# Seven block products for the upper halves too in slices 11 to 14, two more fast steps, and the FFN's input made in another way

## The chip, the cores and the metric

The kernel runs on one core of one Trainium2 chip. The metric is device time in microseconds (us), the median of several runs. TensorE (PE) multiplies matrices, VectorE (DVE), ScalarE (ACT) and GpSimd (POOL) work element by element, and SyncE (SP) issues the DMA transfers, among them transposing ones.

## The reference

Three layers follow each other on 2304 tokens of 512 features (4 batches x 576 positions). The first is linear attention with 8 heads: softmax of q over the head's features, softmax of k over the positions, then q (k^T v). The second is a mixture of 8 experts in which all experts work on all tokens:

```python
P = np.exp(logits)                      # (2304, 8), balanced in 8 rounds over rows and columns
for e in range(E):
    h = np.maximum(x @ w1[e], 0.0)      # 512 -> 1024
    out += P[:, e:e + 1] * (h @ w2[e])  # 1024 -> 512
```

The third is a feed-forward layer (FFN) with a gate:

```python
h = x @ w_in                            # 512 -> 2048
g = h * np.clip(h + 3.0, 0.0, 6.0) / 6.0
return g @ w_out                        # 2048 -> 512
```

All arrays are f32.

## The kernel before

**Numbers in two halves.** Each f32 value on TensorE's way is two f16 values, an upper half (its rounding to f16) and a lower half (the rest). Of a product's four cross terms three are computed: upper x upper, upper x lower, lower x upper.

**Tiles and steps.** The tokens are 18 tiles of 128 (index j), six groups of three tiles (384 tokens), and three pairs of groups, `PAIRS`. The hidden features are cut into 20 slices s of 512: 0 to 15 are the experts' (`NE` = 16, two a expert), 16 to 19 the FFN's. A step (s, p) is one slice for one pair, 60 steps in all; `turns[s]` says in which order a slice takes the pairs (0,1,2 for odd slices and 16, mostly 2,1,0 for the others).

**First layer of a step (`ups`).** The product of x and w1 goes by Strassen's and Winograd's seven block products: 84 matmuls of 384 columns. Their results (banks x, y, z) are read by ACT and DVE into f32 tiles t[1] to t[4] (`ring_r`), put through relu, and split into an upper half (ACT) and a lower half (GpSimd or DVE), both in `ring_h`.

**Second layer (`downs`).** While a step's first layer runs, TensorE also works off the second layer of the step before, in pieces between the products. A plain step does it by `down_tile`: per token tile 12 matmuls of 512 columns, 72 a step, and one DVE operation that adds bank x factor to `acc` (128x512, all tokens stay in SBUF). In slices `FAST` (2 to 14 and 17 to 19) `downs_fast` takes a tile of both groups of the pair together, three times a step: `cross` forms seven block products of 4 matmuls of 256 columns for the two mixed terms, and `main` adds the upper x upper term in full, 8 matmuls of 256 and 4 of 512. The seven products need sums of the hidden features, `s_sums` (S, eight a step, one DVE operation on 128x768 f16 each, upper and lower halves summed apart), and sums of w2, `t_sums` (T1 to T4, once a slice, DVE on f16). ACT copies parts of banks on ("seeds"), and `onto` adds to `acc` by three DVE operations per tile. In the rows S appears as `xbuf<-ring_h`, T1 as scr, T2 as kvs, T3 as xbuf, T4 as xbuf and lg.

**Weights.** A slice's w1 and w2 come by DMA into one shared f32 buffer, `raw`, are scaled by a power of two and split into w1buf and w2buf (two of each). `when` says in which step they are asked for: w1 of the next slice in the first step of a slice, w2 in the second.

**The FFN's input.** When the mixture is done for a pair, in the steps after slice 15's last pieces, `x2_steps(p)` finds the largest value (`across_max`, with a small product by an identity), scales two groups of `acc` in place on ACT (`scaled`, 128x1536), takes three differences, and makes seven forms, each: upper half on ACT, lower half on GpSimd (three of them) or DVE, into one of three staging tiles in scr, then a transposing DMA on SP's queue into x's slot. For pairs 0 and 2 a store of the whole slot to DRAM (`xkeep`, 128x5376) ends the steps; seven loads (`reload`) bring x back in later slices.

**Order.** All operations are first recorded by a planner, which gives each a latest time by what needs it, lays every engine's list out in order of those times (an operation may stand up to `LEAD` = 40 us ahead of where the program recorded it, and "fill" operations such as weight work go where an engine has room), and then issues them. All of it is issued by line 469, so that nearly all rows of the profile carry L469. Each engine then works its list strictly in order. DVE and GpSimd aren't laid at the same time where they would share a port.

The lines that the change touches: `s_sums` and `t_sums` (1430, 1445), `down_tile` (1582), `ups` with its u0 to u6, `downs_fast` (from 1795), `x2_steps` (1944), `when` (2102), `after` (2155).

Of the kernel before, what the change touches and what calls it, by code (L numbers as in the profile page):

```python
# [71 lines left out]
class Planner:  # L72
# [23 lines left out]
    def __init__(self, nc):  # L96
# [5 lines left out]
        self.filling = False  # L102
        self.loose = 0.0
# [102 lines left out]
    def add(self, eng, name, a, k):  # L206
# [85 lines left out]
    def order(self):  # L292
# [14 lines left out]
        for o in ops:  # L307
            o["late"] -= EARLIER.get(o["mark"], 0.0)
# [5 lines left out]
    def lay(self, ops, first):  # L314
# [158 lines left out]
def tile_attention_moe_ffn(  # L473
# [30 lines left out]
    FAST = [*range(2, 15), *range(17, 20)]  # L504
    PAIRS = [(0, 1), (3, 4), (2, 5)]
# [86 lines left out]
    xs = [xbuf[:, i * X_W : (i + 1) * X_W] for i in range(len(PAIRS))]  # L592
    U = [scr[:, i * GN : (i + 1) * GN] for i in range(8)]
# [204 lines left out]
    def w2_steps(s, flat=raw):  # L798
# [12 lines left out]
        return steps + [sp(c) for c in range(NFC)]  # L811
# [618 lines left out]
    def s_sums(hs, which, qf):  # L1430

        a11, a12, a21, a22 = hs[1].get(qf + 2), hs[1].get(qf), hs[0].get(qf + 2), hs[0].get(qf)
        for k in which:
# [4 lines left out]
            elif k == 2:  # L1438
                nc.vector.tensor_sub(o, hs[2][1, qf], a11)
            elif k == 3:  # L1440
                nc.vector.tensor_sub(o, a11, a21)
            else:
                nc.vector.tensor_sub(o, a12, hs[2][2, qf])

    def t_sums(s, which):
        w = w2op[s % 2]
# [3 lines left out]
        for k in which:  # L1450
# [13 lines left out]
    def up_burst(s, p, qf, hs, between):  # L1464
# [57 lines left out]
        if not ffn:  # L1522
# [21 lines left out]
            if s in FAST:  # L1544
# [26 lines left out]
        if s in FAST:  # L1571
# [10 lines left out]
    def down_tile(s, p, grp, t, hs):  # L1582
        w = w2op[s % 2]
        g = PAIRS[p][grp]
        j = g * GJ + t
        ps = bank_of("d", [P, DM])
        ts_ = slice(t * P, (t + 1) * P)
# [7 lines left out]
        cf = factor(s, p, j)  # L1595
# [55 lines left out]

    def ups(s, p, hs):
# [3 lines left out]
        fast = s in FAST and (s, p) != order[-1]  # L1656
# [59 lines left out]
        def burst(qf):  # L1716
# [44 lines left out]
            def u5():  # L1761
# [6 lines left out]
                if fast:  # L1768
                    after_units(5, lambda: s_sums(hs, (3, 1), qf))
                    after_units(6, lambda: s_sums(hs, (2,), qf))  # L1770

            def u6():
# [11 lines left out]
                if fast:  # L1784
                    after_units(6, lambda: s_sums(hs, (4,), qf))
# [475 lines left out]
```

## Time and profile before

| | us |
|---|---|
| median of three runs | 1796.35 |
| the three runs | 1795.88, 1796.35, 1800.01 |
| the profiled execution, its own time | 1798.6 |
| its span, first to last instruction | 1796.8 |
| TensorE busy | 1773.1 (99%) |
| DVE, ACT, GpSimd busy | 1281.7, 1156.4, 551.5 |

The profile is of one execution; times inside it count from the first instruction. A step's start is the first matmul of 384 columns of its first layer. Slice 11 starts at 1003.71, slice 15 at 1340.51, step (16,0) at 1428.44 and (16,1) at 1457.26. The shown length of a matmul includes its way through the array, so what one costs in a stream is the distance of two starts.

### The profile page before, as it was taken

How to read it: one execution, taken by the hardware profiler on the slowest of the kernel's cores; microseconds unless marked ns; L12 is line 12 of the kernel's file. 1: busy time of each engine (PE TensorE's matmuls, PEld its weight loads, DVE VectorE, ACT ScalarE, POOL GpSimd, SP SyncE). 2: the span in 40 equal slices, each digit the busy share in tenths (PEclk: the TensorE clock that was granted, in tenths of full speed). 3: DMA queues.
4: the chain of work that ended last, by engine and by line, in shares of the span. 5: the costliest groups of instructions: out<-in, count | busy, mean ns of one | idle time of the engine just before them, and what ended most of it. 6: DMA issues, size and time to landing. Idle time of an engine off the chain costs nothing.

```text
span 1796.8 us, 32664 instructions
## 1 busy us (share of the span) xinstructions
PE 1773.1 (99%) x12917; PEld 1192.9 (66%) x12917; DVE 1281.7 (71%) x2379; ACT 1156.4 (64%) x2546; POOL 551.5 (31%) x530
## 2 busy tenths in 40 slices
PE   7999999999999999999999999999999989999999
PEld 5555556777777777777777777777776545577775
DVE  6874776787787778786867666665756786778774
ACT  5856575666676667676766666666656676776553
POOL 3423244323333242323232222222222433232221
PEclk9999999999999999999999999999999999999999
DMA  8410231423142323232322212020202563202031
GB/s 271 136 68 1 86 103 42 124 74 127 59 139 77 115 82 116 83 106 89 108 82 72 71 39 85 25 85 25 85 25 85 139 128 112 85 24 86 1 97 71
DMA packets 101593, 154.16 MB, mean 86 GB/s; under 512 B 47552, under 2 KB 51648, under 8 KB 100928
## 3 DMA queue, kind: packets, MB, share of 16 engines
q1 hardware_dynamic: 101440, 152.08, 27.1%
q8 instruction: 101, 1.65, 0.4%
q14 instruction: 52, 0.43, 0.1%
HBM read 119.69 MB, written 24.12 MB: 80 GB/s over the span
## 4 chain that ended last, share of the span: by engine, by line
PE 96%; DMA 1%; DVE 1%; ACT 1%; issue 1%; SPq 0%; POOL 0%; DVEq 0%
PE b L469 95%; PE b L2227 0%; DMA raw<-in_moe_w_dram 0%; DMA acc<-in_v_dram 0%; DMA xbuf<-in_k_dram 0%; DMA acc<-in_q_dram 0%; DVE acc L469 0%; ACT acc L469 0%; DVE prob L469 0%; SPq L469 0%; DVE ring_x2m L469 0%; DVE ring_c L469 0%; ACT ring_r L469 0%; ACT scr L469 0%; DVE ring_r L469 0%
## 5 line engine op out<-in xcount | busy, mean ns | idle before, releaser
L469 PE MATMUL b<-xbuf,w1buf 128*128 128x384 f16 x5040 | 906.6, 326 | 5.8 <-ACT ring_r L469 3.7
L469 PEld LDWEIGHTS <-w1buf 128*128 128x128 f16 x5040 | 492.3, 98 | 289.1 <-issue 7.9
L469 PE MATMUL b<-w2buf,ring_h 128*128 128x256 f16 (+1 forms) x3756 | 683.7, 315 | 0.0
L469 POOL TENSOR_TENSOR ring_h<-ring_r,ring_h 128x384 f16<-128x384 f32 x360 | 342.1, 952 | 1020.9 <-ACT ring_h L469 829.1
L469 PEld LDWEIGHTS <-ring_h 128*128 128x128 f16 x4320 | 422.1, 98 | 194.8 <-issue 3.0
L469 ACT COPY b<-b 128x256 f32<-128x256 f32 (+1 forms) x658 | 240.7, 374 | 291.8 <-PE b L469 193.3
L469 DVE SCALAR_TENSOR_TENSOR acc<-b,ring_cf,acc 128x512 f32<-128x512 f32 x369 | 275.3, 749 | 210.0 <-PE b L469 194.8
L469 ACT ACTIVATE ring_r<-b 128x384 f32<-128x384 f32 x432 | 210.9, 489 | 177.5 <-PE b L469 170.7
L469 PEld LDWEIGHTS <-xbuf 128*128 128x128 f16 x2436 | 225.0, 98 | 76.7
L469 DVE SCALAR_TENSOR_TENSOR ring_r<-b,ring_r 128x384 f32<-128x384 f32 x282 | 155.9, 553 | 119.2 <-ACT ring_r L469 58.1
L469 ACT ACTIVATE ring_h<-ring_r 128x384 f16<-128x384 f32 x330 | 168.8, 521 | 13.6 <-DVE ring_r L469 8.6
L469 DVE TENSOR_TENSOR xbuf<-ring_h 128x768 f16<-128x768 f16 x188 | 115.9, 617 | 1.7 <-POOL ring_h L469 1.7
L469 PE MATMUL b<-xbuf 64*64 64x65 f32 (+1 forms) x1140 | 96.8, 253 | 1.9 <-issue 1.2
L469 PE MATMUL b<-scr,xbuf 128*128 128x256 f16 x564 | 84.6, 273 | 0.0
L469 PE MATMUL b<-w2buf,xbuf 128*128 128x256 f16 x564 | 84.6, 273 | 0.0
L469 PE MATMUL b<-kvs,xbuf 128*128 128x256 f16 x564 | 84.6, 273 | 0.0
L469 ACT CAST ring_h<-ring_r 128x384 f16<-128x384 f32 x150 | 75.0, 508 | 10.4 <-DVE ring_r L469 9.5
L469 DVE SCALAR_TENSOR_TENSOR acc<-b,ring_co,acc 128x512 f32<-128x512 f32 x78 | 58.0, 748 | 32.2 <-PE b L469 30.2
L469 DVE SCALAR_TENSOR_TENSOR w1buf<-raw,ring_ws,w1buf 128x512 f16<-128x512 f32 x100 | 73.6, 768 | 3.0 <-ACT w1buf L469 2.4
L469 ACT ACTIVATE ring_r<-ring_r 128x384 f32<-128x384 f32 x114 | 59.6, 523 | 19.9 <-DVE ring_r L469 19.5
L469 ACT ACTIVATE w1buf<-raw,ring_ws 128x512 f16<-128x512 f32 x100 | 67.6, 714 | 6.1 <-DVE ring_ws L469 4.8
L469 DVE SCALAR_TENSOR_TENSOR ring_h<-ring_r,ring_h 128x384 f16<-128x384 f32 x96 | 63.9, 666 | 10.0 <-ACT ring_h L469 8.9
(167 smaller groups left out, 1554.7 us busy)
## 6 DMA issues: line engine op xcount, KB each, us to landing
xbuf<-xkeep SPq DMA_DIRECT2D x119, 384.0 KB, 3.7
raw<-in_moe_w_dram SPq DMA_DIRECT2D x31, 1024.0 KB, 6.5
xkeep<-xbuf SPq DMA_DIRECT2D x4, 2688.0 KB, 8.6
scr<-in_moe_w_in_dram SPq DMA_DIRECT2D x16, 512.0 KB, 3.6
scr<-in_moe_w_out_dram SPq DMA_DIRECT2D x16, 512.0 KB, 3.4
out_dram<-acc SPq DMA_DIRECT2D x18, 256.0 KB, 2.0
win<-scr SPq DMA_DIRECT2D x16, 256.0 KB, 2.6
wout<-scr SPq DMA_DIRECT2D x16, 256.0 KB, 2.1
```

Source lines behind the costliest of these rows:

```text
L469: f(*a, **k)
```

## The change

1. In slices `FULL` (11 to 14) `cross` takes all three terms through the seven products (6 matmuls each), and `main` does nothing. The sums S are made in f32 from the hidden tiles themselves (`whole`), in place, and then split, upper half on ACT and lower on DVE; the tiles take turns in twelve rooms (six of `ring_r`, six in scr). The sums of w2 are made in f32 in `raw` by four GpSimd operations and then split. One lower half per quarter (in `u6`) goes from GpSimd to DVE, with relu folded into its ACT operation. `raw` is thus in use longer, and `when` asks for the weights one step later in slices next to `FULL` ones.
2. The steps (15,0) and (16,2) (`ALSO`) also go by `downs_fast`. `onto` copies with ACT where `acc` is touched first.
3. x2: the scaling in place is gone. Each form scales while it makes its upper half, and its lower half is two DVE operations on 128x384, all seven on DVE. The store into `xkeep` is seven pieces, asked for after slice 16's steps (`keep`), and isn't laid ahead of its place (`patient`).
4. The very last token tile is cut in 384 and 128 columns, with a bank each.

The core of the diff:

```diff
+    ALSO = ((15, 0), (16, 2))
+    FULL = range(11, 15)
...
+        if s in FULL:
+            b11, b12, b21, b22 = w2_parts
+            steps += [lambda a=a: nc.gpsimd.tensor_sub(*a) for a in ((b11, b12, b11), (b12, b22, b12), (b22, b11, b22))]
+            steps += [lambda: nc.gpsimd.tensor_add(b21, b21, b22)]
...
     def t_sums(s, which):
+        if s in FULL:
+            b11, b12, b21, b22 = w2_parts
+            for k in which:
+                o, part = {1: (T1, b11), 2: (T2, b22), 3: (T3, b12), 4: (T4, b21)}[k]
+                split(o[0], o[1], part, res[s]["s2"][:, 0:1])
+            return
...
+        if (s, p, grp, t) == (*order[-1], 1, GJ - 1):
+            for cols in (slice(0, 3 * DM // 4), slice(3 * DM // 4, DM)):
+                ps = bank_of("d", [P, DM])[:, cols]
...
             def tile_(n):
-                t[n] = rt(f"r{n}_{s}_{p}_{qf}")
+                if full and rooms[0] % 12 > 5:
+                    t[n] = scr[:, rooms[0] % 12 % 6 * GN : (rooms[0] % 12 % 6 + 1) * GN]
+                else:
+                    t[n] = rt(f"r{n}_{s}_{p}_{qf}")
+                rooms[0] += 1
                 return t[n]
+
+            def whole(which):
+
+                for k in which:
+                    o = hs[2][k, qf] = sview[sums[0] % SN]
+                    sums[0] += 1
+                    if k == 1:
+                        r = t[1]
+                        nc.vector.tensor_add(r, t[4], r)
...
+                    else:
+                        r, other = (t[3], t[1]) if k == 2 else (t[4], t[4])
...
+                            nc.vector.scalar_tensor_tensor(
+                                out=r, in0=t[3], scalar=0.0, in1=other, op0=ALU.max, op1=ALU.subtract
+                            )
+                    nc.scalar.copy(o[:, 0, :], r)
+                    nc.vector.tensor_sub(o[:, 1, :], r, o[:, 0, :])
...
+                    if full:
+                        lo(hi(t[2], 1, qf, True), t[2], True)
+                        return
                     nc.scalar.activation(t[2], t[2], AF.Relu)
                     lo(hi(t[2], 1, qf, False), t[2], False)
...
             def cross(o, a, b, first=False):
...
+                terms = [(qf, x, y) for qf in range(2) for x, y in ((0, 1), (1, 0), (0, 0))[: 3 if whole_sums(s, p) else 2]]
...
             def main(o, grp, cols):
+                if whole_sums(s, p):
+                    return
...
-                nc.scalar.copy(o[:, 0], src)
-                eng.tensor_sub(o[:, 1], src, o[:, 0])
+                nc.scalar.activation(o[:, 0], src, AF.Copy, scale=by)
+                for c in range(2):
+                    eng.scalar_tensor_tensor(
+                        out=o[:, 1, c], in0=src[:, c], scalar=by, in1=o[:, 0, c], op0=ALU.mult, op1=ALU.subtract
+                    )
...
-            scaled(gb), sub(xtmp, b22, b12), form(QB22, b22, G), scaled(ga), sub(b12, b12, b11), form(QB11, b11, V),
-            sub(b22, b22, b12), form(QT3, xtmp, V), form(QB21, b21, G), form(QT1, b12, V),
-            sub(b21, b21, b22), form(QT2, b22, G), form(QT4, b21, V),
+        steps = [sub(xtmp, b22, b12), sub(b12, b12, b11)] + steps + [
+            form(QB22, b22, V), form(QB11, b11, V),
+            sub(b22, b22, b12), form(QT3, xtmp, V), form(QB21, b21, V), form(QT1, b12, V),
+            sub(b21, b21, b22), form(QT2, b22, V), form(QT4, b21, V),
         ]
-        if p in xkeep:
-            steps.append(lambda: nc.sync.dma_start(out=xkeep[p], in_=xs[(2, 1, 0)[p]]))
...
+    def keep(p, room):
+        n = X_W // 7
+        for i in range(7):
+            c = slice(i * n, (i + 1) * n)
+            nc.patient = True
+            nc.sync.dma_start(out=xkeep[p][:, c], in_=room[:, c])
+            nc.patient = False
...
-    when = {(s, turns[s][n]): ["w1", "w2"][n : n + 1] for s in range(2, NS - 1) for n in range(2)}
+    when = {
+        (s, turns[s][n + (s in FULL or s + 1 in FULL)]): ["w1", "w2"][n : n + 1]
+        for s in range(2, NS - 1) for n in range(2)
+    }
```

What it does to the order of instructions: first VectorE where step (11,2) ends and (12,2) begins, before. b_67 and b_66 are the banks of `onto`, b_65 the bank n1 and b_62 the bank y; `xbuf<-ring_h` is a sum S.

```order
L469 SCALAR_TENSOR_TENSOR acc<-b_67,ring_cf,acc 128x512
L469 SCALAR_TENSOR_TENSOR acc<-b_66,ring_cf,acc 128x512
L469 TENSOR_TENSOR xbuf<-ring_h 128x768
L469 TENSOR_TENSOR xbuf<-xbuf,ring_h 128x768
L469 TENSOR_TENSOR xbuf<-ring_h 128x768
L469 TENSOR_TENSOR xbuf<-ring_h,xbuf 128x768
L469 SCALAR_TENSOR_TENSOR acc<-b_65,ring_cf,acc 128x512
L469 SCALAR_TENSOR_TENSOR ring_r<-b_62,ring_r 128x384
L469 TENSOR_TENSOR ring_wsc<-ring_ws 128x1
L469 TENSOR_SCALAR ring_cf<-prob,ring_wsc 128x18
L469 SCALAR_TENSOR_TENSOR acc<-b_65,ring_cf,acc 128x512
L469 SCALAR_TENSOR_TENSOR ring_h<-ring_r,ring_h 128x384
```

The same place after the change.

```order
L471 TENSOR_TENSOR ring_r<-ring_r 128x384
L471 TENSOR_SCALAR ring_c1i<-ring_c_109 128x1
L471 TENSOR_SCALAR ring_ws<-ring_c1i 128x1 x2
L471 SCALAR_TENSOR_TENSOR ring_r<-b_62,ring_r 128x384
L471 SCALAR_TENSOR_TENSOR ring_r<-ring_r 128x384 x2
L471 SCALAR_TENSOR_TENSOR acc<-b_67,ring_cf,acc 128x512
L471 SCALAR_TENSOR_TENSOR acc<-b_66,ring_cf,acc 128x512
L471 TENSOR_TENSOR xbuf<-ring_r,xbuf 128x384 x2
L471 SCALAR_TENSOR_TENSOR ring_h<-ring_r,ring_h 128x384
L471 TENSOR_TENSOR xbuf<-ring_r,xbuf 128x384
L471 SCALAR_TENSOR_TENSOR ring_r<-ring_r 128x384
L471 SCALAR_TENSOR_TENSOR w2buf_82<-raw,ring_ws,w2buf_82 128x512 x2
```

Four f16 sums stood behind the two evictions from b_67 and b_66; now f32 operations in place (ring_r<-ring_r) stand ahead of the evictions, and the subtractions that make lower halves of S (`xbuf<-ring_r,xbuf`) behind them, with a lower half of h and w2 splits between.

SP's queue around the FFN's input, before. xkeep_96 is the store of pair 0 and xkeep_97 that of pair 2, win and wout are the FFN's weights.

```order
L469 DMA_TRANSPOSE xbuf<-scr 128x12x128
L469 DMA raw<-win_98 128x4x512
L469 DMA_TRANSPOSE xbuf<-scr 128x12x128 x6
L469 DMA xkeep_96<-xbuf 128x5376
L469 DMA_TRANSPOSE xbuf<-scr 128x12x128 x7
L469 DMA raw<-wout_99 128x4x512
L469 DMA_TRANSPOSE xbuf<-scr 128x12x128 x7
L469 DMA xkeep_97<-xbuf 128x5376
L469 DMA raw<-win_98 128x4x512
L469 DMA xbuf<-xkeep_96 128x768 x7
```

The same place after the change.

```order
L471 DMA_TRANSPOSE xbuf<-scr 128x12x128 x7
L471 DMA raw<-win_98 128x4x512
L471 DMA_TRANSPOSE xbuf<-scr 128x12x128 x14
L471 DMA raw<-wout_99 128x4x512
L471 DMA xkeep_96<-xbuf 128x768 x7
L471 DMA raw<-win_98 128x4x512
L471 DMA raw<-wout_99 128x4x512
L471 DMA xkeep_97<-xbuf 128x768 x7
L471 DMA xbuf<-xkeep_96 128x768 x7
```

The store of pair 0 stood between the transposes of two pairs; now it stands behind all 21 transposes, in seven pieces.

## Rows read from the trace of the kernel before

**Rows 1.** The page, part 1: busy time, share and instructions of each engine.
```profile
PE 1773.1 (99%) x12917; PEld 1192.9 (66%) x12917; DVE 1281.7 (71%) x2379; ACT 1156.4 (64%) x2546; POOL 551.5 (31%) x530
```

**Rows 2.** Waits of TensorE, whole span: total us, times, longest us.
```profile
PE b L469 <- DVE scr L469: 6.5, 2, 6.4
...
PE b L469 <- ACT ring_r L469: 3.7, 2, 3.0
```

**Rows 3.** Timeline of TensorE in slice 11: start, us, operation, count.
```profile
1003.71 2.11 PE L469 MATMUL b<-xbuf,w1buf 128*128 128x384 f16 x12
1005.66 0.60 PE L469 MATMUL b<-w2buf,ring_h 128*128 128x256 f16 x4
1006.09 2.11 PE L469 MATMUL b<-xbuf,w1buf 128*128 128x384 f16 x12
...
1013.49 1.03 PE L469 MATMUL b<-w2buf,ring_h 128*128 128x512 f16 x4
1014.35 0.38 PE L469 MATMUL b<-w2buf,xbuf 128*128 128x256 f16 x2
```

**Rows 4.** Windows: length, busy PE, PEld, DVE, ACT, POOL (count), clock, DMA share, GB/s.
```profile
1003.71:1087.91 84.20, 84.20 (x617) 59.98 (x614) 54.25 (x100) 52.79 (x123) 21.44 (x23) 1.00 0.19 59
496.10:582.48 86.38, 86.38 (x633) 61.58 (x631) 68.81 (x122) 59.34 (x137) 31.92 (x30) 1.00 0.34 112
1428.44:1457.26 28.82, 28.12 (x154) 14.74 (x151) 24.39 (x42) 20.88 (x33) 11.42 (x8) 1.00 0.79 190
1457.26:1493.43 36.17, 31.32 (x158) 15.79 (x158) 27.95 (x59) 28.00 (x49) 11.99 (x10) 0.95 0.58 126
1493.43:1522.62 29.19, 29.19 (x157) 15.27 (x156) 19.16 (x34) 19.55 (x39) 13.48 (x12) 1.00 0.31 119
```

**Rows 5.** Groups by form, VectorE, slices 11 to 14: count, busy us, mean ns, idle before.
```profile
L469 DVE TENSOR_TENSOR xbuf<-ring_h 128x768 f16<-128x768 f16 x48 | 27.7, 577 | 0.0
...
L469 DVE SCALAR_TENSOR_TENSOR ring_h<-ring_r,ring_h 128x384 f16<-128x384 f32 x24 | 17.1, 714 | 4.2 <-ACT ring_h L469 3.7
...
L469 DVE SCALAR_TENSOR_TENSOR w2buf<-raw,ring_ws,w2buf 128x512 f16<-128x512 f32 x16 | 11.6, 747 | 2.0 <-ACT w2buf L469 2.0
```

**Rows 6.** The same for ACT.
```profile
L469 ACT ACTIVATE ring_h<-ring_r 128x384 f16<-128x384 f32 x96 | 49.0, 522 | 3.4 <-DVE ring_r L469 1.5
...
L469 ACT ACTIVATE w2buf<-raw,ring_ws 128x512 f16<-128x512 f32 x16 | 10.6, 713 | 0.4
```

**Rows 7.** Timeline of VectorE where step (12,2) begins.
```profile
1085.94 0.56 DVE L469 SCALAR_TENSOR_TENSOR ring_r<-b,ring_r 128x384 f32<-128x384 f32 x1 [0.56 <-PE b L469]
1087.24 1.62 DVE L469 SCALAR_TENSOR_TENSOR acc<-b,ring_cf,acc 128x512 f32<-128x512 f32 x2 [0.74 <-PE b L469]
1088.78 0.55 DVE L469 TENSOR_TENSOR xbuf<-ring_h 128x768 f16<-128x768 f16 x1
```

**Rows 8.** Timelines of TensorE and of GpSimd at the same place.
```profile
1092.24 0.60 PE L469 MATMUL b<-kvs,xbuf 128*128 128x256 f16 x4
...
1087.68 0.91 POOL L469 TENSOR_TENSOR ring_h<-ring_r,ring_h 128x384 f16<-128x384 f32 x1 [0.68 <-ACT ring_h L469]
```

**Rows 9.** Timeline of TensorE in step (16,1); in brackets idle before and its releaser.
```profile
1461.32 2.13 PE L469 MATMUL b<-xbuf,w1buf 128*128 128x384 f16 x12 [1.89 <-DMA xbuf<-scr]
1466.40 1.59 PE L469 MATMUL b<-xbuf,w1buf 128*128 128x384 f16 x6 [2.96 <-ACT ring_r L469]
```

**Rows 10.** Timelines of SP's queue and of ACT around the same step.
```profile
1430.86 0.32 SPq L469 DMA_DIRECT2D xkeep<-xbuf  x1
1432.80 26.24 SPq L469 DMA_TRANSPOSE xbuf<-scr  x7
...
1460.50 1.58 ACT L469 ACTIVATE acc<-acc,sx 128x1536 f32<-128x1536 f32 x1 [2.56 <-DVE sx L469]
```

**Rows 11.** Groups by form, VectorE, whole span: lower halves of the x2 forms.
```profile
L469 DVE TENSOR_TENSOR scr<-acc,scr 128x768 f16<-128x768 f32 x9 | 9.1, 1009 | 0.0
```

**Rows 12.** Timeline of VectorE at the end of the span.
```profile
1793.13 0.75 DVE L469 SCALAR_TENSOR_TENSOR acc<-b,ring_co,acc 128x512 f32<-128x512 f32 x1 [1.84 <-PE b L469]
```

More of the change, by code (lines that the diff above doesn't have):

```diff
@@ L1585, in down_tile @@
         j = g * GJ + t
+        ts_ = slice(t * P, (t + 1) * P)
+        cf = factor(s, p, j)
+        if (s, p, grp, t) == (*order[-1], 1, GJ - 1):
+            for cols in (slice(0, 3 * DM // 4), slice(3 * DM // 4, DM)):
+                ps = bank_of("d", [P, DM])[:, cols]
+                for n in range(12):
+                    fc, (hi, wi) = (0, 2, 1, 3)[n // 3], ((0, 0), (0, 1), (1, 0))[n % 3]
+                    nc.tensor.matmul(ps, hs[grp][fc][:, hi, ts_], w[:, wi, fc, cols], start=(n == 0), stop=(n == 11))
+                nc.vector.scalar_tensor_tensor(
+                    out=acc[:, j, cols], in0=ps, scalar=cf, in1=acc[:, j, cols], op0=ALU.mult, op1=ALU.add
+                )
+            leave(s, j)
+            return
         ps = bank_of("d", [P, DM])
-        ts_ = slice(t * P, (t + 1) * P)
         n = 0
@@ L1655, in ups @@
         x = slot(s, p)
-        fast = s in FAST and (s, p) != order[-1]
+        fast = quick(s, p) and (s, p) != order[-1]
+        full = fast and whole_sums(s, p)
         ffn = s >= NE
@@ L1838, in onto @@
                 a = acc[:, j, :].rearrange("p (i n) -> p i n", n=hw)
-                nc.vector.scalar_tensor_tensor(
-                    out=a, in0=ps, scalar=factor(s, p, j), in1=a, op0=ALU.mult, op1=ALU.add
-                )
+                key = (j, s >= NE)
+                if key not in started:
+                    started.add(key)
+                    nc.scalar.activation(a, ps, AF.Copy, scale=factor(s, p, j))
+                else:
+                    nc.vector.scalar_tensor_tensor(
+                        out=a, in0=ps, scalar=factor(s, p, j), in1=a, op0=ALU.mult, op1=ALU.add
+                    )
             def p1():
@@ L1904, in begin @@
             d0[5]()
-        new = s != prev[0] and s in FAST
+        new = s != prev[0] and quick(s, p)
         T = lambda k: (lambda: t_sums(s, k) if new else None)
@@ L1961, in x2_steps @@
         )
[L1963 to L1964 removed]
+        by = sx[:, p, 0:1]
         def sub(o, u, v):
@@ L2160, in after @@
             if ps_ == NE - 1:
-                run(loosely(x2_steps(pp), X2_LATE[pp]))
+                run(marked(f, f"x2{pp}") for f in loosely(x2_steps(pp), X2_LATE[pp]) if f is not None)
                 done.add(("x2", pp))
+            if ps_ == NE and pp in xkeep:
+                keep(pp, xs[(2, 1, 0)[pp]])
     put(ticks, w1_1[4:])
@@ L2206, in tile_attention_moe_ffn @@
             all_conv()
-        fast = prev is not None and prev[0] in FAST
+        fast = prev is not None and quick(*prev[:2])
         if laid and not fast:
```

92 lines of the change are left out of this document (61 added, 31 removed).

## The prediction

> **What bounds the kernel now.** I read the page's first part first, then TensorE's waits, then the timeline and the windows of the stages that the change touches. TensorE is busy 1773.1 us of the span [rows 1], so all its idle time together is 23.7 us, and most of the named waits are elsewhere: 6.5 us while the kernel starts, and 5.6 us (3.7 behind ACT and 1.9 behind a transfer) between slices 15 and 16 [rows 2, 9]. In slices 11 to 14 it has none: slice 11 is 84.20 us with 84.20 busy [rows 4]. There the time is the number of matmuls times their spacing, and a slice gets shorter only if matmuls go or get narrower, as long as VectorE (DVE), at 54.25 us, keeps up.
>
> The spacing comes from the starts. Twelve matmuls of 384 columns take 1005.66 - 1003.71 = 1.95 us, so 162.5 ns each; four of 512 take 1014.35 - 1013.49 = 0.86 us, so 215 ns [rows 3]. For 256 columns I take the slice as a whole: 84.20 less 252 x 0.1625 and less 36 x 0.215 leaves 35.5 us for 324 matmuls, 109.6 ns each; the four at 1005.66 agree (0.43 us) [rows 3, 4].
>
> **Seven products for upper halves (slices 11 to 14).** Per token tile and pair of groups TensorE now issues 7 x 4 matmuls of 256 and for the upper halves 8 of 256 and 4 of 512: 36 x 0.1096 + 0.86 = 4.81 us. After the change it is 7 x 6 = 42 of 256: 4.60 us. That is -0.203 us, times 3 tiles, 3 pairs and 4 slices (36): **-7.3 us**, all on the path, because TensorE has no idle time there.
>
> What this costs beside TensorE: each of the 24 sums of a slice was one f16 operation of 577 ns at most [rows 5], and is now one f32 operation of 384 columns on DVE, one ACT copy and one DVE subtraction to f16. Neighbouring DVE operations start some 0.5 us apart, though each shows 0.55 (1088.78, 0.55, in a row of four) [rows 7], so a 384-column operation counts about 0.51, and a sum gains 0.51 us: 24 x 0.51 = 12.2. Six lower halves move from ACT and GpSimd to ACT and DVE, some 0.6 each by the row at 714 with its contention [rows 5]: 3.6. The four sums of w2 become four splits of 747 ns in place of five f16 sums; I take that as even. So DVE has 54.25 + 15.8 = 70 us in a slice of 84.20 - 1.8 = 82.4 (85%); with 714 ns for every subtraction and 0.56 for every f32 operation it is 77 (93%). Slice 5 runs today at 68.81 of 86.38 (80%) with TensorE never idle [rows 4]. ACT: 24 - 6 operations of 522 ns and four of 713 [rows 5, 6] add 12.2 to 52.79, 79%. By the totals both engines have room; the order decides.
>
> The tight place is the start of a step. DVE finishes its last read of a product at 1085.94 + 0.56, evicts two banks from 1087.24, makes the four sums from 1088.78, and TensorE first uses one at 1092.24 [rows 7, 8]. The changed order puts the f32 parts ahead of the two evictions and the subtractions behind them. Three subtractions from 1088.78 at 0.51 to 0.71 are done by 1090.3 to 1090.9, 1.3 us or more before 1092.24. The in-place f32 operation must however wait for GpSimd to have read its tile (a lower half ends there at 1087.68 + 0.91 = 1088.6 [rows 8]); then the two evictions (1.62) and three subtractions (1.5 to 2.1) stand behind it on the same engine: with the f32 operation 1088.6 + 0.56 + 1.62 + 1.5 to 2.1 = 1092.3 to 1092.9, up to 0.7 us late. I take **+1.0 us** over the twelve steps (the subtractions mostly in time, as the order puts GpSimd's reads early), with 0 and 12 x 0.7 = +8.4 as ends; a gain below 0 is excluded, since TensorE has nothing idle there to give back.
>
> **Slices (15,0) and (16,2) fast.** A plain step has 72 matmuls of 512 in its second layer, 72 x 0.215 = 15.48; a fast one 3 x 4.81 = 14.42. Two of them: **-2.1 us**. It adds eight f16 sums (some 0.5 each) and three evictions to DVE in each of the two steps.
>
> **The boundary of 15 and 16: x2 redone.** Here TensorE is idle 28.82 - 28.12 = 0.70 and 36.17 - 31.32 = 4.85 us, and the second window has a granted clock of 0.95, 36.17 x 0.05 = 1.8 us at the 1.2 GHz level behind the idle time; together 7.35 us to be had [rows 4]. The wait at 1461.32 is for a transposing DMA, the one at 1466.40 for ACT, which has scalings of 1.58 us on 128x1536 in its order there [rows 9, 10]. The store of x stands on SP's queue at 1430.86, directly ahead of the seven transposes of the next pair, which then take from 1432.80 to 1459.04 to be issued [rows 10]. The change takes both causes away: the scalings are folded into the forms, and in the changed order the store comes behind all transposes of the next two pairs.
>
> What it adds there is DVE work: seven forms with two half-width operations each, 14 x 0.51 to 0.71 = 7.1 to 10 us, in place of four subtractions of 1.009 [rows 11], since three were on GpSimd: +3.1 to +6 per pair, I take +4.5. DVE has 24.39 + 27.95 + 19.16 = 71.5 us in the three windows from 1428.44 to 1522.62 [rows 4]; with two pairs (9), the sums and evictions of (16,2) (some 6) it has 86.5, and if the whole 7.35 us came back there would be 94.2 - 7.35 = 86.8 for it. DVE would have to be full for three steps, in an order that also waits. So I take half, **-3.7 us**, between 0 and -7.35.
>
> **Last tile.** The final tile's product is cut into 384 and 128 columns. TensorE's total stays (12 x 0.215 against 12 x (0.1625 + about 0.054)); after its last matmul only 128 columns are to be added instead of 512, which took 0.75 us [rows 12]. By 0.56 for 384 columns some 0.3 remain: **-0.4 us**.
>
> **Sum.** -7.3 - 2.1 - 3.7 - 0.4 + 1.0 = -12.5 us. The profiled execution took 1798.6 us (1796.8 of span), 2.25 above the median of the three runs, so 1798.6 - 12.5 = 1786.1 on its scale is **1783.9 us** on the median's. The small edits (when a weight is asked for, first touches of the output on ACT, sign of a sum) are counted at nothing: raw is held one step longer, and by the order the next weights are still asked for a step (28 us) ahead of their first use. If that cover is gone, the first step of a slice waits.
>
> **Rivals.** (a) Nothing comes back at the boundary: DVE, fuller by 4.5 us a pair, becomes what TensorE waits for. For: the account above is full to 0.3 us. Against: most of the work may slide into the lighter steps before and after. 1783.9 + 3.7 = 1787.6 us.
>
> (b) The sums are late at each step's start by the 0.7 us worked out above. For: DVE takes its work in order, and waits for GpSimd where it did not. Against: 1.3 us of slack if GpSimd is early. 1783.9 + 7.4 = 1791.3 us.
>
> (c) Slower: DVE bounds the twelve steps. If it waits for every ACT copy before its subtraction with nothing in between, a sum costs 0.56 + 0.52 + 0.57 = 1.65 us instead of 0.51: 9.1 us more per step, and 1.2 for the lower halves, on the 18.1 us (54.25 / 3) of now: 28.4; two waits of 0.91 for GpSimd make it 30.2 against TensorE's 27.5. 12 x 2.7 = 32 us, so 1815 us. It decides from about 29.0 us a step (1.5 us late), where the sum passes +0.3%. Against: the changed order puts evictions and other tiles' work between copy and subtraction.
>
> (d) The narrow matmuls cost more than their columns in the new, longer groups of six. A tile costs 4.81 us before, so seven products pay only while one of 42 takes less than 4.81 / 42 = 0.1145 us; the rows show 0.1096 in groups of four [rows 3, 4], and eight percent would have to come from the grouping alone. At 0.1145 the 7.3 us are gone: 1783.9 + 7.3 = 1791.2 us. Nothing in the rows speaks for it; 1 in 100.
>
> The Trainium skill, page "TensorE: Matmul & The Clock Gate", section "Back-to-back issue gap", speaks against the change here: in a stream of weight loads and matmuls the sustained spacing is about 81 ns for 128 columns and 131 ns for 512, and the isolated formula N / 2.4 + 2.5 overstates wide ones. An estimate from that page (98 ns for 256 columns, between its two) would make a tile 4.05 us before and 4.12 after, +2.3 us over the 36 instead of a gain. This case's rows disagree, with 215 ns for 512 columns in just such a stream.
>
> **Chances.** Forecast and its own spread (1779 to 1787): 0.60; (a) 0.18; (b) 0.15, about half of it within the bound; (c) 0.04; (d) 0.01; that the weights, taken later, hold up a step so that most of the gain goes: 0.02. A measurement of this kernel tells about 0.3% (5.4 us) from no change, so faster means under 1791.0 and slower over 1801.7: faster 0.85, same 0.11, slower 0.04. The range goes from everything recovered (1783.9 - 3.65 - 1.0 = 1779.2, less some scatter: 1778.5) up to (b) with a little: 1792.
>
> **What would show it.** In the changed trace slices 11 to 14 should be 82.4 us, with DVE at 68 to 77 and no wait of TensorE for DVE; a row of waits behind a sum (xbuf) in those slices is (b), DVE above 80 is (c). Between 15 and 16 the transposes should no longer be spread over 26 us, ACT shows no scaling of 1.58 us, and idle time plus half clock should be about half of 7.35 us; if idle time there is behind DVE, it is (a). The steps after (15,0) and (16,2) should be 28.1 where plain ones are 29.1. The prediction is wrong if slices 11 to 14 do not get shorter by 1.8 us each, or if another boundary grows.

## The result, and the profile after

The changed kernel takes 1780.49 us, the median of five runs (1779.69 to 1781.37); before it were 1796.35. The ratio is 0.9905, with a 95% interval of 0.9891 to 0.992: faster, by 15.9 us, 3.4 us more than forecast and inside the range. All medians below are of fast runs; of e1 one run in four, at 3782.23 us, counts as slow and is left out. The profiled execution took 1781.37 us, its span is 1779.6.

The page's first part (after), which answers to [rows 1]: TensorE has 20.3 us of idle time in the span, against 23.7, and 1759.3 us of busy time, against 1773.1. So most of the gain is busy time that went; the table below says how much of that is matmuls and how much the lower clock.

```profile
PE 1759.3 (99%) x13097; PEld 1208.3 (68%) x13097; DVE 1377.2 (77%) x2550; ACT 1193.9 (67%) x2654; POOL 543.4 (31%) x513
```

Windows of the kernel after, columns as in [rows 4]: slices 12 and 13, steps (15,0) and (15,2), then the steps (16,0), (16,1) and (16,2).

```profile
1084.00:1166.57 82.57, 82.49 (x635) 61.73 (x632) 69.92 (x127) 61.68 (x147) 22.83 (x20) 1.00 0.20 60
1166.57:1248.89 82.32, 82.32 (x633) 61.74 (x632) 69.66 (x128) 61.40 (x147) 23.14 (x20) 1.00 0.20 60
1331.22:1360.03 28.81, 27.62 (x214) 20.61 (x211) 25.92 (x47) 21.70 (x52) 10.80 (x9) 1.00 0.27 83
1389.42:1418.67 29.25, 29.25 (x159) 15.33 (x157) 25.87 (x46) 14.47 (x25) 4.76 (x5) 1.00 0.63 124
1418.67:1447.92 29.25, 29.25 (x160) 15.33 (x158) 27.62 (x50) 16.68 (x30) 9.27 (x8) 1.00 0.52 98
1447.92:1478.07 30.15, 29.46 (x160) 15.39 (x159) 29.05 (x64) 23.06 (x39) 7.63 (x7) 1.00 0.58 97
1478.07:1507.69 29.62, 29.62 (x160) 15.50 (x159) 25.09 (x49) 23.73 (x48) 9.99 (x9) 1.00 0.49 164
```

Slices 12 and 13 last 82.57 and 82.32 us, where they were 84.20; VectorE is busy 69.9 and 69.7 us of that, ACT 61.7. Step (16,1) lasts 30.15 us instead of 36.17, at a granted clock of 1.00 instead of 0.95. Step (15,0) has 1.19 us without TensorE that weren't there before. Where a step starts among the pieces of the second layer has moved too, so single steps don't compare well: (15,1) takes 29.39 us, not the 28.1 that the prediction expected behind (15,0), but (15,1) and (15,2) together take 58.64 where they took 59.84.

TensorE's waits (after) from slice 11 to the end of slice 16, in all:

```profile
PE b L471 <- ACT ring_r L471: 1.2, 1, 1.2
PE b L471 <- DVE ring_r L471: 0.7, 1, 0.7
```

The first is the new wait in (15,0); the second, in (16,1), is what is left of the 5.6 us that [rows 2, 9] show there. From the start of slice 11 to the end of the span the traces differ by 793.09 - 777.32 = 15.8 us (1796.8 - 1003.71 and 1779.6 - 1002.28; before slice 11 they differ by 1.4, of which 1.2 arose in the first 243 us, which the change leaves alone). The 15.8 us split like this; matmuls are counted with the distance of starts in the longest runs of one width, the same in both traces (20 of 256 columns in 2.18 us, 109.2 ns each, and 12 of 512 in 2.59 us, 215.8 ns each):

| part | forecast, us | measured, us | from |
|---|---|---|---|
| FULL, matmuls | -7.3 | -7.5 | 36 x (4.794 - 4.586) |
| FULL, waits | +1.0 | +1.3 | 1.19 in (15,0) and 0.08 in slice 12 (82.57 - 82.49) |
| fast steps (15,0) and (16,2) | -2.1 | -2.3 | 2 x (15.54 - 14.38), matmuls |
| boundary of 15 and 16 | -3.7 | -6.7 | idle 5.55 to 0.69, and the 1.8 that the 1.2 GHz level cost |
| last tile | -0.4 | -0.3 | start of (19,0) to the end: 47.44 to 47.19 |
| sum | -12.5 | -15.5 | of 15.8; 0.3 are not assigned |

The start of step (12,2), which answers to [rows 7, 8]. TensorE's first use of a sum, VectorE ahead of it, and GpSimd's lower half that the f32 operation in place has to wait for (all after):

```profile
1089.87 0.82 PE L471 MATMUL b<-kvs,xbuf 128*128 128x256 f16 x6
1090.52 0.82 PE L471 MATMUL b<-xbuf 128*128 128x256 f16 x6
```

```profile
1084.67 1.14 DVE L471 SCALAR_TENSOR_TENSOR ring_r<-ring_r 128x384 f32<-128x384 f32 x2
1085.91 1.41 DVE L471 SCALAR_TENSOR_TENSOR acc<-b,ring_cf,acc 128x512 f32<-128x512 f32 x2
1087.24 1.02 DVE L471 TENSOR_TENSOR xbuf<-ring_r,xbuf 128x384 f16<-128x384 f32 x2
1088.17 0.55 DVE L471 SCALAR_TENSOR_TENSOR ring_h<-ring_r,ring_h 128x384 f16<-128x384 f32 x1
1088.64 0.55 DVE L471 TENSOR_TENSOR xbuf<-ring_r,xbuf 128x384 f16<-128x384 f32 x1
```

```profile
1083.04 0.91 POOL L471 TENSOR_TENSOR ring_h<-ring_r,ring_h 128x384 f16<-128x384 f32 x1 [3.65 <-ACT ring_h L471]
```

GpSimd's lower half ends at 1083.95, ahead of the operations in place at 1084.67, so that wait costs nothing here. Two sums' subtractions end at 1088.26, and TensorE uses the first at 1089.87: 1.6 us of slack, where 1.3 or more was forecast for the case of an early GpSimd.

The wait in (15,0) is the one place in slices 11 to 15 where the new sums hold TensorE. Timelines of TensorE, ACT, VectorE and GpSimd there (after):

```profile
1342.69 1.14 PE L471 MATMUL b<-xbuf,w1buf 128*128 128x384 f16 x6 [1.19 <-ACT ring_r L471]
```

```profile
1342.14 0.49 ACT L471 ACTIVATE ring_r<-b 128x384 f32<-128x384 f32 x1 [1.38 <-DVE xbuf L471]
```

```profile
1340.38 1.73 DVE L471 TENSOR_TENSOR xbuf<-ring_r,xbuf 128x384 f16<-128x384 f32 x2
```

```profile
1340.44 1.25 POOL L471 TENSOR_TENSOR ring_h<-ring_r,ring_h 128x384 f16<-128x384 f32 x1 [1.34 <-ACT ring_h L471]
```

Read backwards: TensorE waits for a bank that ACT reads; ACT's read at 1342.14 waited 1.38 us for VectorE, since the f32 tile that it writes was still the source of a sum's subtraction; the two subtractions took 1.73 us instead of 1.02 (1087.24 above), beside a GpSimd operation that took 1.25. That 0.7 us more is over half of the 1.19. FULL steps have twelve rooms for these tiles; by the diff an ordinary step such as (15,0) takes only the six of `ring_r`, so it comes back to a room sooner.

SP's queue around x2 (after), which answers to [rows 10]: all 21 transposes stand ahead of the first piece of the store (xkeep). The 14 are two sevens of 21.7 and 20.5 us, where they took 26.2 and 25.0. With the store put back (e2) the first of these sevens takes 22.1, so the store made little of the spread that the prediction put beside it.

```profile
1396.97 17.17 SPq L471 DMA_TRANSPOSE xbuf<-scr  x7
1414.19 0.90 SPq L471 DMA_DIRECT2D raw<-win  x1
1425.25 49.74 SPq L471 DMA_TRANSPOSE xbuf<-scr  x14
1478.92 0.38 SPq L471 DMA_DIRECT2D raw<-wout  x1
1479.35 4.59 SPq L471 DMA_DIRECT2D xkeep<-xbuf  x7
```

The x2 groups on VectorE, steps (15,2) to (16,2), after and then before: the new lower halves (36 of 42 in one group), and the differences on 128x768.

```profile
L471 DVE SCALAR_TENSOR_TENSOR scr<-acc,sx,scr 128x384 f16<-128x384 f32 x36 | 23.3, 692 | 0.0
...
L471 DVE TENSOR_TENSOR acc<-acc 128x768 f32<-128x768 f32 x9 | 8.8, 980 | 0.1
```

```profile
L469 DVE TENSOR_TENSOR acc<-acc 128x768 f32<-128x768 f32 x9 | 10.9, 1213 | 1.8 <-ACT acc L469 1.8
```

VectorE's last operations in the span (after), which answer to [rows 12]: two operations, 384 and 128 columns, 1.02 us together in place of 0.75, but the span ends sooner, because the first runs beside the last matmuls.

```profile
1775.50 1.02 DVE L471 SCALAR_TENSOR_TENSOR acc<-b,ring_co,acc 128x384 f32<-128x384 f32 x2 [1.20 <-PE b L471]
```

### The profile page after: what moved, and what is told of

Same layout as the page of the kernel before. It is cut to its first block, busy times and chain, and to the rows that moved or that the text cites. A ratio compares the mean times of both kernels' runs of the same rounds, so it can differ in the third digit from the quotient of the medians.

```text
span 1779.6 us, 33317 instructions
## 1 busy us (share of the span) xinstructions
PE 1759.3 (99%) x13097; PEld 1208.3 (68%) x13097; DVE 1377.2 (77%) x2550; ACT 1193.9 (67%) x2654; POOL 543.4 (31%) x513
## 4 chain that ended last, share of the span: by engine, by line
PE 96%; DVE 2%; DMA 1%; ACT 0%; issue 0%; SPq 0%; POOL 0%; ACTq 0%; POOLq 0%
PE b L471 96%; DMA acc<-in_v_dram 0%; DMA raw<-in_moe_w_dram 0%; DVE xbuf L471 0%; DMA xbuf<-in_k_dram 0%; DMA acc<-in_q_dram 0%; DVE ring_r L471 0%; PE b L2331 0%; DVE prob L471 0%; DVE ring_c L471 0%; DVE ring_h L471 0%; DVE ring_qm L471 0%; DVE scr L471 0%; SPq L471 0%; DVE acc L471 0%
## 5 line engine op out<-in xcount | busy, mean ns | idle before, releaser
L471 PE MATMUL b<-w2buf,ring_h 128*128 128x256 f16 (+1 forms) x3456 | 608.5, 310 | 0.1
L471 POOL TENSOR_TENSOR ring_h<-ring_r,ring_h 128x384 f16<-128x384 f32 x312 | 299.5, 962 | 876.5 <-ACT ring_h L471 727.3
L471 PEld LDWEIGHTS <-ring_h 128*128 128x128 f16 x4116 | 401.2, 98 | 171.6 <-issue 2.1
L471 PEld LDWEIGHTS <-xbuf 128*128 128x128 f16 x2820 | 262.9, 98 | 77.3
L471 ACT ACTIVATE ring_r<-b 128x384 f32<-128x384 f32 x384 | 187.5, 489 | 141.7 <-PE b L471 135.4
L471 PE MATMUL b<-xbuf 128*128 128x256 f16 (+1 forms) x1236 | 107.3, 249 | 4.1 <-issue 1.7
L471 DVE TENSOR_TENSOR xbuf<-ring_h 128x768 f16<-128x768 f16 x148 | 91.4, 620 | 0.0
L471 DVE SCALAR_TENSOR_TENSOR acc<-b,ring_co,acc 128x512 f32<-128x512 f32 (+1 forms) x82 | 60.5, 742 | 30.7 <-PE b L471 27.6
L471 PE MATMUL b<-xbuf,ring_h 128*128 128x256 f16 x366 | 80.0, 273 | 0.0
L471 PE MATMUL b<-lg,ring_h 128*128 128x256 f16 x294 | 74.1, 273 | 0.0
```

What stands on the lines that cost most here:

```text
L471: f(*a, **k)
```

## The experiments

Each kernel was timed in three rounds or more beside the kernel before on the same chip; a ratio is to that kernel. The medians come from several chips, so differences of medians are rough. Traces are compared from the start of slice 11 to the end of the span, which leaves out the kernel's start (it differs by some us between executions of one program): 793.1 us before, 777.3 after. That column is from one execution of each kernel. The intervals of e2 and e3 reach into that of the changed kernel, so that they cost anything rests on their traces.

| kernel | median, us | ratio to before (95%) | slice 11 to end, against after |
|---|---|---|---|
| after | 1780.49 | 0.9905 (0.9891 to 0.992) | 0 |
| e1 FULL out | 1788.81 | 0.9953 (0.9936 to 0.997) | +8.0 |
| e2 store put back | 1784.16 | 0.9921 (0.9905 to 0.9938) | +4.4 |
| e3 forms put back | 1784.73 | 0.9927 (0.9911 to 0.9943) | +2.3 |
| e10 fast steps out | 1784.80 | 0.9941 (0.9926 to 0.9956) | +4.5 |
| e7 before, new forms | 1796.03 | 1.0001 (0.9989 to 1.0013) | +14.3 |
| e8 before, store moved | 1797.27 | 1.0005 (0.9993 to 1.0017) | +15.8 |
| e9 before, both | 1796.35 | 1.0008 (0.9995 to 1.0021) | +15.0 |
| e4 VectorE, 24 more a slice | 1821.42 | 1.013 (1.0115 to 1.0145) | +41.4 |
| e5 VectorE, 6 more a slice | 1789.25 | 0.9959 (0.9942 to 0.9976) | +8.0 |
| e12 ACT, 24 more a slice | 1800.61 | 1.0033 (1.0017 to 1.0049) | +20.6 |
| e6 slices 11 to 13 | 1788.16 | 0.9944 (0.9924 to 0.9964) | +5.1 |
| e11 slices 10 to 14 and 19 | 1777.58 | 0.9902 (0.9886 to 0.9919) | -3.3 (from step (9,2) on) |

### Parts undone one by one

**e1: the seven products for upper halves out.**

```diff
-    FULL = range(11, 15)
+    FULL = ()
```

> The changed kernel with the seven products for upper halves taken out again (no slice in FULL; weights are asked for as before), all other parts kept. Theory: the twelve FULL steps gave 36 x 0.208 = 7.5 us of matmuls and lost about 1.3 us in waits (1.19 us at the start of step (15,0)), so this runs at 1780.5 + 6.2 = 1786.7 us, slices 11 to 14 at 84.2 us each and no wait in (15,0). Rival: the fuller VectorE of slices 11 to 14 also pushes work into the boundary of 15 and 16; then the boundary is shorter here too and the time stays under 1785.5.

Windows of e1, step (16,1):

```profile
1453.18:1485.20 32.02, 30.18 (x160) 15.25 (x158) 29.86 (x64) 23.94 (x40) 7.24 (x7) 1.00 0.57 104
```

(With FULL empty `when` also asks for the weights of slices 11 to 15 as before.) The time is 1788.81 us, more than either theory gave. Slices 11 to 14 are back at 84.20 us each and (15,0) has no wait, which is the expected 6.2. The rest is at the boundary: 32.02 us with 1.84 idle in step (16,1), against 30.15 with 0.69. So the sums don't burden the boundary; without them it got worse. Why is not shown: the planner lays out the whole list anew.

**e2: the store as one transfer behind its pair's transposes.**

```diff
+        if p in xkeep:
+            steps.append(lambda: nc.sync.dma_start(out=xkeep[p], in_=xs[(2, 1, 0)[p]]))
         return steps
...
-            if ps_ == NE and pp in xkeep:
-                keep(pp, xs[(2, 1, 0)[pp]])
```

> The changed kernel with the store of x2 (xkeep) put back as one transfer behind the transposes of its pair, as before; forms stay new. Theory Q (the queue: the store ahead of the next pair's transposes made the wait): the idle time in step (16,1) comes back, 4 to 7 us with the low clock behind it, 1784.5 to 1787.5 us. Theory F (the forms: scalings on ACT and lower halves on GpSimd made it): no change, within 1 us of 1780.5, and the transposes still wait behind the store without TensorE noticing.

TensorE's timeline of e2 in (16,1), the two longest waits:

```profile
1454.24 1.14 PE L471 MATMUL b<-xbuf,w1buf 128*128 128x384 f16 x6 [1.03 <-DVE ring_r L471]
1456.66 0.23 PE L471 MATMUL b<-identb,ring_c 128*128 128x128 bf16 x1 [1.28 <-DVE ring_c L471]
```

4.4 us by the trace, 3.7 by the medians. Waits and the lower clock come back in (16,1), as theory Q had it: 34.46 us, 2.8 of them idle, at a granted clock of 0.95. But the idle time is less than its 4 to 7 us, and the longest waits are behind VectorE, not behind a transfer.

**e3: the forms as before** (`scaled` on ACT, three lower halves on GpSimd; the lines are those of the diff above, taken back).

> The changed kernel with the seven forms of x2 made as before (scaled in place on ACT, three lower halves on GpSimd), the store kept at its later place. Theory Q: within 1 us of 1780.5. Theory F: the idle time in step (16,1) comes back, 4 to 7 us, 1784.5 to 1787.5 us. If both this and the store put back cost several us, either cause alone was enough to make the wait.

TensorE's timeline of e3 in (16,1), the two longest waits:

```profile
1456.30 1.14 PE L471 MATMUL b<-xbuf,w1buf 128*128 128x384 f16 x6 [0.85 <-DVE ring_r L471]
1458.64 1.14 PE L471 MATMUL b<-xbuf,w1buf 128*128 128x384 f16 x6 [1.21 <-ACT ring_r L471]
```

2.3 us by the trace and about 4 by the medians; (16,1) takes 32.44 us, 2.6 of them idle, at a granted clock of 1.00. By the traces both e2 and e3 cost several us, so each part is needed; neither theory alone is right.

**e10: the two fast steps out.**

```diff
-    ALSO = ((15, 0), (16, 2))
+    ALSO = ()
```

> The changed kernel with (15,0) and (16,2) plain again. Theory (matmul count only): 2 x 1.15 = 2.3 us more, 1782.8 us, the wait in (16,1) still under 1 us. Rival (the boundary hangs on every step near it): a wait of 2 us or more with the low clock behind it comes back in (16,1), 1785 us or more.

TensorE's timeline of e10, waits in slice 16:

```profile
1426.48 1.14 PE L471 MATMUL b<-xbuf,w1buf 128*128 128x384 f16 x6 [0.41 <-DVE ring_r L471]
...
1452.81 1.14 PE L471 MATMUL b<-xbuf,w1buf 128*128 128x384 f16 x6 [1.41 <-DVE ring_r L471]
...
1483.91 1.14 PE L471 MATMUL b<-xbuf,w1buf 128*128 128x384 f16 x6 [0.77 <-ACT ring_r L471]
```

4.5 us by the trace: 2.3 are the matmuls, most of the rest are waits of 0.4, 1.4 and 0.8 us in slice 16 where there was one of 0.7. Neither theory gave this: the matmuls and a smaller wait than the rival's.

### The x2 parts alone, on the kernel before

**e7: new forms only. e8: store moved only. e9: both.** Their edits are the parts of the diff above on `form`, on `keep`, and both, made in the kernel before.

> The kernel before with one part of the change: the seven forms of x2 scale by themselves, all lower halves on VectorE; the store stays where it was. From the two undoings: the forms are worth 2.3 us by the trace, the store's place 4.3. If the two causes add, this gains 2.3 us (1794 us, the wait in step (16,1) at about 4 us with the low clock behind it). Rival (either cause alone keeps the whole wait, and only both together free it): within 1 us of before.

> The kernel before with one part of the change: the store of x2 in seven pieces after slice 16's steps, the forms as before. If the two causes add: 4.3 us less than before (1792 us), the idle time of step (16,1) down from 5.55 to about 2.6 us. Rival (only both together free it): within 1 us of before.

> The kernel before with both parts of the x2 change (forms and the store's place), without the seven products for upper halves, the two fast steps and the split last tile. Each part alone gave nothing measurable (0 +- 2 us). Theory (they free the wait only together): idle time in step (16,1) under 2.5 us, 1791.5 us or less. Rival (it takes the new order that the other parts bring as well): within 2 us of before, idle time in (16,1) still 4 us or more.

The longest wait of TensorE in (16,1), of e7, e8 and e9 in this order:

```profile
1458.73 0.23 PE L469 MATMUL b<-identb,ring_c 128*128 128x128 bf16 x1 [2.80 <-DVE ring_c L469]
```

```profile
1467.48 1.46 PE L470 MATMUL b<-xbuf,w1buf 128*128 128x384 f16 x6 [4.25 <-ACT ring_r L470]
```

```profile
1458.30 0.29 PE L470 MATMUL b<-identb,ring_c 128*128 128x128 bf16 x1 [2.80 <-DVE ring_c L470]
```

None moves the time (1.0001, 1.0005, 1.0008). Taking away both causes that [rows 9, 10] name puts another wait in their place: in e7 and e9 TensorE waits 2.80 us for the small product by the identity that spreads a pair's largest value (`identb`, behind VectorE's `ring_c`), with the lower clock behind it as before. The window of step (16,1) of e9 has a granted clock of 0.95:

```profile
1453.39:1489.22 35.83, 31.31 (x159) 15.71 (x158) 31.66 (x71) 24.39 (x45) 7.10 (x7) 0.95 0.50 107
```

What stands on VectorE around it shows in the splits of w1 from raw, e9 and then after (count, shortest/median/longest ns, first and last start):

```profile
L470 DVE SCALAR_TENSOR_TENSOR w1buf<-raw,ring_ws,w1buf x5: 742/746/747, 1449.2 to 1457.4; 128x512 f16<-128x512 f32 x5
```

```profile
L471 DVE SCALAR_TENSOR_TENSOR w1buf<-raw,ring_ws,w1buf x10: 737/745/1403, 1473.1 to 1529.9; 128x512 f16<-128x512 f32 x10
```

In e9 five splits of slice 17's w1 stand from 1449.2 to 1457.4, in the step's first 4 us and just before it, ahead of that wait. In the changed kernel they begin at 1473.1 (the row counts those of slice 18 too), 25 us into the step, since the diff also asks for the weights of slice 17 one step later:

```diff
+    for n in range(3):
+        when[NE, turns[NE][n]] = [(), ("w1",), ("w2",)][n]
```

This is in e1, e2, e3 and e10, whose step (16,1) takes 30.8 to 34.5 us, and not in e7 to e9, where it takes 35.8 to 37.0 (36.17 before). The fast steps, with their first touches of the output on ACT, are not in e10, and the new sums are not in e1, so neither is what (16,1) needs. That the time of the weights is the part that frees the boundary is argued from these traces; it wasn't tried by itself.

### How much room the sums have

**e4 and e5: the sums' last VectorE operation twice, for all sums or for one in four; e12: their ACT copy twice.** The same values are written again, so that only time is added. The edit of e5; e4 does the same for every k, and e12 repeats `nc.scalar.copy` instead:

```diff
-                    nc.vector.tensor_sub(o[:, 1, :], r, o[:, 0, :])
+                    for _ in range(2 if k == 2 else 1):
+                        nc.vector.tensor_sub(o[:, 1, :], r, o[:, 0, :])
```

> The changed kernel with the subtraction of every f32 sum's lower half done twice (the same value written again), 24 more VectorE operations of some 0.47 us per slice: VectorE from 69.7 to 81 us in slices of 82.3 (98%). Theory (TensorE sets the pace as long as the totals have room, the order is loose): 0 to 5 us more, 1780.5 to 1785.5. Rival c of the prediction (VectorE's order binds well before it is full): slices 11 to 14 grow to 85 us or more, over 10 us more, above 1790.5 us.

> The changed kernel with the lower-half subtraction done twice for one of the four sums only (k = 2): 6 more VectorE operations per slice, some 0.47 us each, VectorE 69.7 to 72.5 us in 82.3 (88%). With all four doubled the kernel took 41 us more, with idle time up to 7 us in one step and the low clock behind it. Theory (a threshold: there is slack of some 1 to 2 us per step, beyond which waits grow): 0 to 3 us more, 1780.5 to 1783.5. Rival (a slope from the first operation on: a quarter of the load, a quarter of the price): 10 us more, 1790.5.

> The changed kernel with the ACT copy of every f32 sum done twice (the same value written again): 24 more ACT operations of some 0.42 us per slice, ACT from 61.5 to 71.6 of 82.3 us (87%). A doubled VectorE subtraction cost 41 us for 24 operations and 9 us for 6. Theory (VectorE, in its order, is what is tight): 0 to 6 us more, 1780.5 to 1786.5. Rival (the length of the chain from the f32 sum to TensorE is tight, whichever engine it runs on): 20 us more or above, 1800 us.

TensorE's waits from slice 11 through (15,0) (the two largest), and then windows of slices, for e4:

```profile
PE b L471 <- DVE xbuf L471: 11.8, 9, 2.3
PE b L471 <- ACT ring_r L471: 9.3, 8, 2.1
```

```profile
1083.13:1172.58 89.45, 83.64 (x633) 61.55 (x632) 80.21 (x153) 61.16 (x145) 34.60 (x20) 1.00 0.18 55
1172.58:1266.89 94.31, 86.93 (x635) 62.87 (x632) 83.75 (x153) 61.48 (x145) 26.55 (x20) 0.96 0.18 53
```

For e5, waits and a window of three steps:

```profile
PE b L471 <- DVE ring_h L471: 2.6, 3, 1.1
PE b L471 <- ACT ring_r L471: 1.9, 3, 0.7
```

```profile
1142.80:1226.06 83.26, 81.12 (x617) 59.80 (x615) 72.05 (x133) 58.99 (x140) 23.50 (x20) 1.00 0.20 59
```

For e12, waits and one window:

```profile
PE b L471 <- ACT b L471: 9.0, 5, 2.7
```

```profile
1174.31:1263.03 88.72, 84.86 (x623) 61.66 (x620) 71.00 (x131) 71.04 (x172) 23.13 (x20) 0.96 0.19 56
```

96 more operations of some 0.47 us (45 us of VectorE) cost 41 us, and 24 (11 us) cost 8 to 9. At these two loads that is some 0.7 to 0.9 us for each us: VectorE was busy 69.7 of 82.3 us, with TensorE never idle in slice 13, and yet had little room for more. A threshold below e5's load, 6 operations a slice, isn't excluded. In e5 VectorE's 72.05 us of 83.26 are 87%, with TensorE idle for 2.1 us of these three steps. `p6` uses the sum that e5 doubles before the others, yet TensorE waits there only 0.5 us for a sum (xbuf) and longer for other work of these engines. The prices of e4 and e12 contain stretches at the lower clock (0.96 in the windows shown). ACT has more: 96 operations of some 0.42 us (40 us) cost 20 us, 13.3 of it in slices 11 to (15,0), behind its copies of banks. The theory for e12 (0 to 6) fell as well, and its rival's 1800 us was met. Yet TensorE waits 9.0 us behind ACT's copies of banks and 0.7 for a sum, which speaks for ACT's fixed order and not for the chain from a sum to TensorE, the rival's reason. The price is on both engines, nearly twice as high on VectorE.

### Where the FULL slices end

**e6: slices 11 to 13.**

```diff
-    FULL = range(11, 15)
+    FULL = range(11, 14)
```

> The changed kernel with the seven products for upper halves only in slices 11 to 13, slice 14 as before. It costs 9 x 0.208 = 1.9 us of matmuls. Theory (the wait of 1.19 us at the start of step (15,0) comes from the weights of the FFN, whose f32 work on GpSimd meets the last FULL sums there): without FULL sums in that step the wait goes, and no such wait appears in (14,0): 1780.5 + 1.9 - 1.2 = 1781.2 us. Rival (each end of the FULL slices costs it): the wait shows in the first step of slice 14 instead, 1782.4 us.

TensorE's timeline of e6, step (14,2):

```profile
1262.01 1.14 PE L471 MATMUL b<-xbuf,w1buf 128*128 128x384 f16 x6 [1.20 <-ACT ring_r L471]
```

ACT's read ahead of it, waiting for the same two subtractions of 1.73 us (e6):

```profile
1261.47 0.49 ACT L471 ACTIVATE ring_r<-b 128x384 f32<-128x384 f32 x1 [1.39 <-DVE xbuf L471]
```

The wait has gone one slice ahead, with the same 1.20 us. So it belongs to the step in which the last f32 sums meet the first ordinary step, and not to the FFN's weights; the rival was right on the place. The time, 1788.16 us, is far above its 1782.4: by the trace it is 5.1 us more than the changed kernel, since the boundary got worse too (3.11 us idle in (16,1)).

**e11: slices 10 and 19 added.**

```diff
-    FULL = range(11, 15)
+    FULL = (*range(10, 15), 19)
```

> The changed kernel with slices 10 and 19 also by seven products for upper halves (10 to 14 and 19). Slice 10 gives 9 x 0.208 = 1.9 us of matmuls, slice 19 two steps, 1.25 us (its last step is plain). VectorE has room in both (busy 54% to 82% of the steps of 10 in the kernel before, some 76% to 81% in 19, where no next weights are made). Theory: 1780.5 - 3.1 = 1777.4 us. Rival (another order at the boundary of 15 and 16, or waits at the ends of the FULL slices, as when a slice was taken out): 1780 us or more, with waits of TensorE that were not there.

Window of e11, step (19,1):

```profile
1702.26:1729.66 27.40, 27.40 (x212) 20.56 (x210) 24.74 (x46) 20.02 (x45) 6.00 (x7) 1.00 0.13 48
```

1777.58 us; by the trace 3.3 us less than the changed kernel from step (9,2) on, with 3.1 expected. Step (19,1) takes 27.40 us instead of 28.03, and no wait appears but the 1.2 at the end of slice 14, 0.3 before it and the 0.7 in (16,1). Against the changed kernel the intervals of the medians overlap (0.9886 to 0.9919 and 0.9891 to 0.992), so that this is better rests on the traces.

## Why the prediction was right, and where it was not

**The matmul count** held. 0.203 us a tile was forecast, and slices 12 and 13 are shorter by 1.6 and 1.9 us (1.8 forecast); e1 loses it again, and e11 gains 3.3 us with five steps more, 3.1 by the count. Spacing by columns, read from starts, is what this part of the kernel costs, as TensorE has no idle time there; the trace shows six matmuls of 256 in 0.65 us (1089.87 to 1090.52), 108 ns each, and 109.2 in longer runs, as in groups of four before. Rival (d) falls with it. For this stream the sustained spacing that the Trainium skill gives (page "TensorE: Matmul & The Clock Gate", section "Back-to-back issue gap") does not hold either: 512 columns take 215.8 ns here, where the page has about 131.

**VectorE in the FULL slices** was forecast at 70 us and measured at 69.7 to 69.9 in slices 12 and 13; ACT was forecast at 65.0 (79%) and measured at 61.4 to 61.7. The slack at the step's start was right as well. The +1.0 us was right in size (1.3) but not in place: it stood for late sums at the starts of the twelve steps, which did not come, and what came is one wait at the end of the FULL slices, for a tile's room, of which no row before spoke. That the size fits is luck.

**Rival (c) was priced too far away.** It was to decide from about 29.0 us of VectorE a step. e4 has 80.2 and 83.8 us in three steps (27 to 28 a step) and is 24 us slower than the kernel before beside it; in e5 waits are there with 6 operations more a slice. What failed there is the reading "by the totals both engines have room": 85% busy looked like 12 us of slack in a slice, and at the points where it counts there was little. The prediction did say that the order decides, but had no row that measured how much the order left. The 4 in 100 for (c) rested on that reading.

**The boundary** is the term that was mis-sized: -3.7 against -6.7. Its 1.8 us are what the 1.2 GHz level cost; TensorE stood at that level for some 3.4 us, behind the wait that ends at 1466.40 [rows 9]. Half was taken because VectorE seemed full: 86.5 of 86.8 us in three steps. It measured 27.62 + 29.05 + 25.09 = 81.8 of 89.0. The new lower halves cost what the upper bound said (692 ns for each); but the differences on 128x768 fell from 1213 to 980 ns, 2.1 us for the nine, and part of the work went into (15,2), where VectorE is busy 25.87 us and was 22.15 in the window before:

```profile
1397.90:1428.44 30.54, 30.54 (x165) 15.89 (x164) 22.15 (x40) 19.63 (x38) 15.51 (x12) 1.00 0.55 115
```

The prediction named that slide into lighter steps as what speaks against (a), and did not price it. As to the mechanism, the two causes that the prediction named (scalings, store) are needed, by the traces of e2 and e3, but not enough (e7 to e9). What was "counted at nothing", when a weight is asked for, is the likeliest third; that it decides is open.

**The fast steps** gave their 2.3 us of matmuls; that leaving them out costs 4.5 was not foreseen. The sum of what the four parts cost when undone one at a time (8.0 + 4.4 + 2.3 + 4.5 = 19.2) is more than the whole change gave (15.8): in e1 and e10 waits at this boundary come on top of the matmuls. **The last tile** came out nearly as forecast.

## What to carry to other kernels

Where the bounding engine is never idle, count its instructions by their distance of starts, and believe that number. A second engine's busy share is no measure of its slack when it works in a fixed order: add a few of its operations and see what they cost, before relying on the rest. At a place where several engines take turns in holding the bound, taking away the waits that the profile names can give nothing until the last of them goes, so try the parts together and undo them one at a time.

## What the runs showed of the hardware

VectorE's operations on two f32 tiles in SBUF can last far longer beside a GpSimd operation. Of the nine differences on 128x768 before, six took 948 to 953 ns and three took 1.33, 1.49 and 2.40 us, each of these beside a GpSimd operation: one beside a lower half of x2, two beside lower halves of hidden features. After, eight took 945 to 957 ns and one, beside GpSimd, 1.22 us. Not every overlap costs: one of the six before and four of the eight after overlap GpSimd's work too. The longest one, and the GpSimd operation in which it starts (both before):

```profile
1449.05 2.40 DVE L469 TENSOR_TENSOR acc<-acc 128x768 f32<-128x768 f32 x1
```

```profile
1448.20 2.43 POOL L469 TENSOR_TENSOR scr<-acc,scr 128x768 f16<-128x768 f32 x1 [1.27 <-ACT scr L469]
```

GpSimd ends at 1450.63, and VectorE 0.82 us behind it, at 1451.45. Two subtractions on 128x384 took 1.73 us beside a GpSimd operation, in (15,0) and again in e6, and 1.02 alone.
